# A second MLP as 2x2 block products with seven multiplications, in superblocks of 768 tokens, with streamed weights

## The chip, the cores and the metric

The kernel runs on one core of one Trainium2 chip. The core has a matrix engine (TensorE: PE in the profile, its weight loads PEld), three elementwise engines (VectorE: DVE, ScalarE: ACT, GpSimd: POOL) and a queue engine (SyncE: SP) from which all DMAs of this kernel are issued. The metric is the device time of one execution in microseconds (us).

## The reference: a retention layer and two MLPs

Retention over 4 batches, 8 heads, 576 positions and 64 dimensions gives a 2304 x 512 matrix. Two MLPs follow, all in float32:

```python
def _moe_ref(x, w_in, w_out):            # x: 2304 x 512, w_in: 512 x 2048, w_out: 2048 x 512
    h = np.maximum(x @ w_in, 0.0)
    return (h * h @ w_out).astype(np.float32)

def _moe2_ref(x, w_in, w_out):
    h = x @ w_in
    relu6 = np.clip(h + 3.0, 0.0, 6.0)
    g = h * relu6 / 6.0
    return (g @ w_out).astype(np.float32)
...
    x = _moe_ref(x=x, **moe_kwargs)
    return _moe2_ref(x=x, **moe2_kwargs)
```

## The kernel before

Every float32 operand of the MLPs is held as two float32r parts, a high one (a rounding cast) and a low one (the rest), and a product is three matmuls: high by high, high by low, low by high. Both MLPs run over the 2304 tokens in five blocks of 512 or 384 (`BLOCKS`), and within a block over 16 slices `f` of 128 hidden features. A step is one `(ph, blk, f)`: `h_part` makes one 128-feature slice of h (12 matmuls, 4 input slices by 3), ACT and DVE turn it into g (`r` at L459 to L463, `g` at L466 to L469), and `a_part` adds the slice's share of the output into PSUM (`acc`, L491 in the first MLP, L493 in the second). The loop over `steps` issues `h_part` of the next step ahead of `a_part` of this one, so that PE has 12 matmuls to do while g is made. The order on every engine is the order in which the program is written; each engine takes its instructions strictly in that order.

The first MLP (`ph` 0) reads its input from SBUF, where `first_*`, `scores` and `values` (the retention, in chunks of 128 tokens, one chunk in four or five steps) have put it for the next block. Its result goes to DRAM (`x1`), and `load_x1` brings it back, block by block, for the second MLP (`ph` 1). Weights come in once per MLP: `load_w` (512 KB per DMA), `scale_w` on ACT (L128, L129) and `narrow_w` on DVE (L144, L145), which turn the 64-bit numbers into float32, and `split_w` (cast on ACT, rest on POOL or DVE, L156 and L158). The 32 weight tiles of an MLP stay in SBUF for all its blocks. The second MLP's weights are prepared during the last block of the first and the first block of the second.

In the second MLP the five blocks take 16 x 12 matmuls each for h (960, moving 512 or 384 columns) and 16 x 3 for each of the 18 groups of 128 tokens (864, moving 512 columns). Each `a_part` result is scaled by 1/6 on its way out (L514 on DVE, L516 on ACT) and stored (L520).

## Time and profile before

| | |
|---|---|
| time, median of 3 runs | 875.69 us (875.45 to 875.77) |
| profiled execution, first to last instruction (the page gives no other time for it) | 874.3 us |
| PE busy | 860.0 us (98%), 5356 matmuls |
| DVE, ACT, POOL busy | 458.5, 227.8, 95.9 us |
| DMA queue of SP | 67.33 MB |

The page divides the span into 40 slices and gives the busy tenths of each engine; a table by stage gives the same in us. The chain that ended last is followed back from the last instruction to what released each step. The profiled execution is one, its span is 1.4 us under the median of the runs.

### The profile page before, as it was taken

To read this page: it belongs to the slowest core of one execution; us is meant where nothing else is said; L and a number is where in the kernel's file an instruction comes from. 1 tells how busy PE (TensorE), PEld (TensorE's weight loads), DVE (VectorE), ACT (ScalarE), POOL (GpSimd) and SP (SyncE) were. 2 spreads that over 40 slices of the span, in tenths; PEclk is the share of its full clock that TensorE was granted. 3 is DMA by queue.
4 is the path that set the end of the run, shared out by engine and by line. 5 is a ranking of instruction groups with operands and counts; after the bars stand their busy time and mean duration, and the time that the engine had idled before them with its cause. 6 is when DMAs were issued, how large, how long until landed. Compare 5 with 4: busy or idle time off the path is not lost.

```text
span 874.3 us, 12831 instructions
## 1 busy us (share of the span) xinstructions
PE 860.0 (98%) x5356; PEld 741.5 (85%) x5356; DVE 458.5 (52%) x778; ACT 227.8 (26%) x394; POOL 95.9 (11%) x86
## 2 busy tenths in 40 slices
PE   8899999999999999999999999999999999999998
PEld 7677779999888899998888998888888888888996
DVE  6788875445444355445788785335333533344333
ACT  2666641111111111114555642111111111111111
POOL 3455560101111011000000000000000000000000
PEclk9999999999999999999999999999999999999999
DMA  9956212112111021016565300100010001001001
GB/s 340 315 203 236 97 49 98 49 49 85 49 49 46 3 96 50 2 38 206 199 213 175 97 13 13 61 1 13 28 57 1 13 35 41 1 10 47 2 1 37
DMA packets 29130, 68.15 MB, mean 78 GB/s; under 512 B 2832, under 2 KB 12176, under 8 KB 29072
## 3 DMA queue, kind: packets, MB, share of 16 engines
q1 hardware_dynamic: 29072, 67.33, 23.2%
q8 instruction: 42, 0.69, 0.3%
q14 instruction: 16, 0.13, 0.1%
HBM read 57.88 MB, written 9.44 MB: 77 GB/s over the span
## 4 chain that ended last, share of the span: by engine, by line
PE 86%; DMA 5%; DVE 3%; issue 2%; POOL 1%; ACT 1%; SPq 0%; POOLq 0%; DVEq 0%; ACTq 0%
PE h L449 41%; PE acc L493 23%; PE acc L491 19%; DMA raw<-w_dram 3%; DMA q<-qk_dram 2%; PE o L420 1%; PE o L410 1%; PE sc L338 1%; POOL w L158 1%; DVE wt L145 1%; DVE wt L144 1%; DVE r L460 0%; PE sc L353 0%; ACT g L466 0%; POOL q L309 0%
## 5 line engine op out<-in xcount | busy, mean ns | idle before, releaser
L449 PE MATMUL h<-x,w 128*128 128x512 f32 (+2 forms) x1932 | 423.4, 367 | 5.8 <-ACT w L156 3.7
L449 PEld LDWEIGHTS h<-x,w 128*128 128x128 f32 x1932 | 351.4, 188 | 56.6 <-ACT w L156 5.7
L491 PE MATMUL acc<-g,w 128*128 128x512 f32 (+1 forms) x960 | 213.7, 371 | 1.0 <-ACT g L466 1.0
L493 PE MATMUL acc<-w,g 128*128 128x512 f32 x864 | 210.2, 391 | 0.3 <-DVE ev L514 0.3
L491 PEld LDWEIGHTS acc<-g,w 128*128 128x128 f32 x960 | 173.5, 188 | 24.3 <-ACT g L466 1.4
L493 PEld LDWEIGHTS acc<-w,g 128*128 128x128 f32 x864 | 161.5, 188 | 33.2 <-DVE ev L514 0.8
L463 DVE SCALAR_TENSOR_TENSOR r<-r,h 128x512 f32<-128x512 f32 (+1 forms) x80 | 50.7, 634 | 203.1 <-ACT r L462 203.0
L462 ACT ACTIVATE r<-h,con 128x512 f32<-128x512 f32 (+1 forms) x80 | 51.7, 646 | 311.3 <-PE h L449 305.8
L460 DVE TENSOR_TENSOR r<-r,h 128x512 f32<-128x512 f32 (+1 forms) x80 | 50.6, 632 | 148.9 <-ACT r L459 148.8
L469 DVE TENSOR_TENSOR g<-r,g 128x512 fp32r<-128x512 f32 (+1 forms) x160 | 108.2, 676 | 16.2 <-ACT g L466 11.2
L459 ACT ACTIVATE r<-h 128x512 f32<-128x512 f32 (+1 forms) x80 | 44.2, 552 | 240.6 <-PE h L449 233.7
L468 DVE CAST g<-r 128x512 fp32r<-128x512 f32 (+1 forms) x144 | 65.1, 452 | 14.6 <-DVE r L460 0.5
L145 DVE CUSTOM_DVE_ANT_0 wt<-raw,wt 128x1024 uint16<-128x1024 uint16 x64 | 47.1, 737 | 4.5 <-DVE wt L144 0.6
L158 POOL TENSOR_TENSOR w<-wt,w 128x512 fp32r<-128x512 f32 x32 | 42.7, 1339 | 53.0 <-ACT w L156 43.9
L128 ACT ACTIVATE raw<-raw 128x512 f32<-128x512 f32 x64 | 42.8, 669 | 2.6 <-DMA raw<-w_dram 2.6
L129 ACT ACTIVATE raw<-raw 128x512 int32<-128x512 uint32 x64 | 42.8, 669 | 0.0
L309 POOL TENSOR_TENSOR q<-q,con 128x512 f32<-128x512 f32 x13 | 18.2, 1402 | 175.7 <-issue 115.7
L156 ACT ACTIVATE w<-wt 128x512 fp32r<-128x512 f32 x50 | 30.8, 627 | 13.3 <-DVE wt L145 13.1
L144 DVE TENSOR_SCALAR wt<-raw 128x512 int32<-128x512 int32 x64 | 30.3, 474 | 0.1
L158 DVE TENSOR_TENSOR w<-wt,w 128x512 fp32r<-128x512 f32 x32 | 21.3, 685 | 0.0
L466 ACT ACTIVATE g<-r 128x512 fp32r<-128x512 f32 x16 | 10.1, 633 | 29.9 <-DVE r L460 29.9
L514 DVE TENSOR_SCALAR ev<-acc 128x512 f32<-128x512 f32 (+1 forms) x18 | 11.8, 658 | 9.1 <-DMA x<-ev 4.1
(47 smaller groups left out, 273.1 us busy)
## 6 DMA issues: line engine op xcount, KB each, us to landing
raw<-w_dram SPq DMA_DIRECT2D x64, 512.0 KB, 5.8
q<-qk_dram SPq DMA_DIRECT2D x17, 512.0 KB, 3.7
kv<-kv_dram SPq DMA_DIRECT2D x30, 256.0 KB, 4.9
out_dram<-ev SPq DMA_DIRECT2D x18, 256.0 KB, 2.1
x<-ev SPq DMA_DIRECT2D x12, 256.0 KB, 2.1
x1r<-x SPq DMA_DIRECT2D x12, 256.0 KB, 4.6
kv<-kv_dram SPq DMA_DIRECT2D x3, 512.0 KB, 7.9
x<-ev SPq DMA_DIRECT2D x8, 192.0 KB, 1.9
```

Of the source, the lines that this page charges most:

```text
L128: nc.scalar.activation(high, high, AF.Prelu, scale=2.0**-112, alpha=-(2.0**32))
L145: nc.vector.tensor_tensor(ti, ti, low, ALU.add)
L158: eng.tensor_tensor(w[:, 1, :], t, w[:, 0, :].bitcast(F32), ALU.subtract)
L449: nc.tensor.matmul(hp[:, ts], w[:, wi, c * P : (c + 1) * P], x[:, xi, c, ts], start=k == 0, stop=k == 3 * NC - 1,)
L459: nc.scalar.activation(r, hp[:, :nb], AF.Relu)
L460: nc.vector.tensor_tensor(r, r, hp[:, :nb], ALU.mult)
L462: nc.scalar.activation(r, hp[:, :nb], AF.Relu, bias=con3)
L463: nc.vector.scalar_tensor_tensor(r, r, 6.0, hp[:, :nb], ALU.min, ALU.mult)
L468: nc.vector.tensor_copy(g[:, 0, :nb], r)
L469: nc.vector.tensor_tensor(g[:, 1, :nb], r, g[:, 0, :nb].bitcast(F32), ALU.subtract)
L491: nc.tensor.matmul(acc[d][:, :nb], wt[:, sl], gt, start=first, stop=stop)
L493: nc.tensor.matmul(acc[d], gt[:, sl], wt, start=first, stop=stop)
```

## The change

Only the second MLP is computed in another way; the first keeps its blocks, steps and matmuls.

- **Seven products.** The tokens are taken in 3 superblocks of 768 (`SUPERS`), each as two halves of 384 (`HALF`). Of both products of the second MLP the operands are cut in 2x2 blocks, seven combinations of each operand are formed, seven block products made, and the four output blocks are sums of those (`ORDER` is the order 1, 6, 7, 5, 2, 4, 3). Two of the sums are made in PSUM, by letting products 2, 4 and 3 add on a bank that already holds 1, 7 or 5.
- **First product.** Per superblock there are 8 pairs `j` of 128 hidden features; per `j` seven products of 6 matmuls, moving 384 columns (L977). Per `j` ACT copies one product out, DVE makes five sums with a PSUM operand (L872), ACT and DVE make the four gated blocks (`relu3` L905, `gate` L908), and POOL four sums of those (`pool_op` L911), which are the seven left operands of the second product (`aop_1` to `aop_7`), kept for all 8 `j`.
- **Second product.** It starts when all 8 `j` are done (h is ahead of it): per superblock 7 x 8 steps of 9 matmuls, moving 256 columns (L1026). `a_cast` (ACT) and `a_low` (DVE, L925) split one 128 x 384 operand per step into six rotating tiles; `merge` and `emit` read the sums out (L939 and the lines behind) and store them.
- **Weights.** Instead of staying in SBUF, the second MLP's combined weights are prepared during the first MLP: 32 `unit`s, each a load (two DMAs), scaling on ACT, narrowing and four sums on DVE, one cast of 128 x 896 on ACT, one subtraction of 128 x 896 on DVE, and two stores of 448 KB to DRAM, in pieces of 512 B. A unit is spread over two steps (`unit_work`), from step 14 of the first block to the end of the first MLP. For every superblock they are read again through a ring of seven 512 KB tiles (`ring_load`): 32 loads for the first product (every fourth 256 KB) and 28 for the second. A tile's next load waits for PE to be done with it.
- **Input.** `x_stages` makes the seven combinations of x1 and their high and low parts for a superblock: for the first one in the last 8 steps of the first MLP, for the others during the second product before.
- **Beside that**, in the first MLP the cast of g to its high part is ACT's in all blocks (before: DVE's after the first block), its low part is emitted behind the unit's DVE work, retention chunks are loaded one ahead instead of two (one buffer instead of two), and a mask is loaded by a DMA of its own.
- The order in the second MLP is set by a list of model times: `at(t, ...)` puts an operation on a heap, and `run(now)` emits what is due as PE's matmuls are written.

```diff
-BLOCKS = (
-    [(512, "xa"), (384, "xb"), (512, "xa"), (384, "xb"), (512, "xa")],
-    [(384, "xb"), (512, "xa"), (512, "xc"), (512, "xa"), (384, "xb")],
-)
+BLOCKS = [(512, "xa"), (384, "xb"), (512, "xa"), (384, "xb"), (512, "xa")]
...
+SUPERS, HALF = 3, 384
...
+ORDER = (1, 6, 7, 5, 2, 4, 3)
...
+RING = 7
...
+    def unit_load(n):
+        i, j, u = n // (2 * NJ), n // 2 % NJ, n % 2
+        raw = upool.tile([P, 2, 2, P, 2], I32, tag="raw", bufs=1, name=f"uraw_{n}")
...
+    def unit_narrow(n):
+        raw = units[n]
+        low, high = raw[:, :, 0], raw[:, :, 1]
+        t = upool.tile([P, 7, P], F32R, tag="seven", bufs=2, name=f"seven_{n}")
+        ti = t[:, :4].bitcast(I32).rearrange("p s n -> p (s n)")
+        nc.vector.tensor_scalar(ti, high, 3, None, ALU.logical_shift_left)
+        nc.vector.tensor_tensor(ti, ti, low, ALU.add)
...
+    def unit_low(n):
+        t, hi = units[n]
+        nc.vector.tensor_tensor(t, t.bitcast(F32), hi.bitcast(F32), ALU.subtract)
+
+    def unit_store(n, x):
...
+        if i == 0:
+            nc.sync.dma_start(w_in_hl[j][:, :, x, cols], part)
+        else:
+            nc.sync.dma_start(w_out_hl[:, :, j, x, cols].rearrange("s p n -> p s n"), part)
+
+    def unit_work(i, slot):
+
+        n, odd = divmod(i, 2)
...
+        if slot == 0 and not odd:
+            on(1, unit_narrow)
+            on(0, unit_load)
+            on(2, unit_store, 0)
+        elif slot == 0:
+            on(2, unit_low)
+            on(2, unit_store, 1)
+        elif not odd:
+            on(1, unit_combine)
+        else:
+            on(0, unit_scale)
+            on(1, unit_cast)
...
+    def ring_load(n):
+        s, i, a, b = ring[n]
+        p = p1c if n % RING == RING - 1 else p1a
+        t = p.tile([P, 2, 2, HALFD], F32R, tag=f"r{n % RING}", name=f"ring_{n}")
...
+            for i, q in enumerate(ORDER):
+                run(now)
+                w = wring[s, 0, j, i // 2][:, i % 2]
+                x = x_ops[q]
...
+                    nc.tensor.matmul(
+                        bank[q],
+                        w[:, wi, u * P : (u + 1) * P],
+                        x[:, u, xi, :],
+                        start=k == 0 and q not in (2, 4, 3),
+                        stop=k == 5,
+                        skip_group_check=q in (2, 4, 3),
+                    )
...
+                    at(now + 2.0, pool_op, 5, 7, 4, ALU.add, j)
+                    at(now + 2.1, pool_op, 7, 1, 7, ALU.subtract, j)
+                    at(now + 2.2, pool_op, 6, 5, 1, ALU.subtract, j)
+                    at(now + 2.3, pool_op, 3, 2, 6, ALU.subtract, j)
...
+                    for m, (g, wi) in enumerate(((0, 0), (0, 1), (1, 0))):
+                        nc.tensor.matmul(
+                            o,
+                            sp[:, g, rows],
+                            w[:, k % 2, wi, :],
```

PE, early in the second MLP before: `h` is a PSUM tile, `x_1_0` the input block, `w_1_f_0` and `w_1_f_1` the two weight tiles of slice f, `acc` the output's PSUM tiles.

```order
L449 MATMUL h_1_0_1_4356<-x_1_0_3999,w_1_1_0_3784 128x384 x12
L493 MATMUL acc_1_0_0_4383<-w_1_0_1_3739,g_1_0_0_4314 128x512 x4
L493 MATMUL acc_1_0_1_4384<-w_1_0_1_3739,g_1_0_0_4314 128x512 x2
L493 MATMUL acc_1_0_0_4383<-w_1_0_1_3739,g_1_0_0_4314 128x512 x2
L493 MATMUL acc_1_0_1_4384<-w_1_0_1_3739,g_1_0_0_4314 128x512
```

PE, the first `j` of the second MLP now: `z0` to `z7` are the eight PSUM banks, `xop_q` the combinations of x, `ring_n` the streamed weights, `spl_s_q_k` the split left operands.

```order
L977 MATMUL z6_4746<-xop_1_4374,ring_0_4428 128x384 x6
L977 MATMUL z7_4747<-xop_6_4375,ring_0_4428 128x384 x6
L977 MATMUL z4_4744<-xop_7_4376,ring_1_4476 128x384 x6
L977 MATMUL z5_4745<-xop_5_4377,ring_1_4476 128x384 x6
L977 MATMUL z6_4746<-xop_2_4378,ring_2_4519 128x384 x6
L977 MATMUL z4_4744<-xop_4_4379,ring_2_4519 128x384 x6
L977 MATMUL z5_4745<-xop_3_4380,ring_3_4571 128x384 x6
```

And PE where the first superblock passes from the first product to the second:

```order
L977 MATMUL z2_4742<-xop_4_4379,ring_30_5153 128x384 x6
L977 MATMUL z3_4743<-xop_3_4380,ring_31_5174 128x384 x6
L1026 MATMUL z6_4746<-ring_32_5192,spl_0_1_0_5233 128x256 x6
L1026 MATMUL z7_4747<-ring_32_5192,spl_0_1_0_5233 128x256 x3
L1026 MATMUL z6_4746<-ring_32_5192,spl_0_1_1_5249 128x256 x6
L1026 MATMUL z7_4747<-ring_32_5192,spl_0_1_1_5249 128x256 x3
```

The two kinds of matmuls that alternated every 12 or 9 now stand in two long runs: 8 x 7 groups of the first kind, then 7 x 8 of the second, and the second kind moves 256 columns instead of 512.

DVE, early in the second MLP before (weights of `ph` 1 still in preparation; `r` reads PSUM), one step:

```order
L158 TENSOR_TENSOR w_1_11_0_4449<-wt_1_11_0_4416,w_1_11_0_4449 128x512
L144 TENSOR_SCALAR wt_1_11_1_4452<-raw_1_11_1_4152 128x512
L145 ISA wt_1_11_1_4452<-raw_1_11_1_4152,wt_1_11_1_4452 128x1024
L463 SCALAR_TENSOR_TENSOR r_1_0_4_4479<-r_1_0_4_4479,h_1_0_4_4466 128x384
L468 CAST g_1_0_4_4482<-r_1_0_4_4479 128x384
L469 TENSOR_TENSOR g_1_0_4_4482<-r_1_0_4_4479,g_1_0_4_4482 128x384
```

DVE now, one `j` of the first product (`held` tiles keep the partial sums, `aop_q` the gated blocks):

```order
L872 TENSOR_TENSOR held0_4710<-z7_4747,held0_4710 128x384
L872 TENSOR_TENSOR held1_4711<-z4_4744,held0_4710 128x384
L872 TENSOR_TENSOR held0_4710<-z5_4745,held1_4711 128x384
L908 SCALAR_TENSOR_TENSOR aop_4_4718<-aop_4_4718,held0_4710 128x384
L908 SCALAR_TENSOR_TENSOR aop_1_4713<-aop_1_4713,z6_4746 128x384
L872 TENSOR_TENSOR held1_4711<-z4_4744,held0_4710 128x384
L872 TENSOR_TENSOR held0_4710<-z5_4745,held0_4710 128x384
L908 SCALAR_TENSOR_TENSOR aop_2_4717<-aop_2_4717,held1_4711 128x384
L908 SCALAR_TENSOR_TENSOR aop_7_4715<-aop_7_4715,held0_4710 128x384
```

Weight preparation, casts and subtractions have left this place; nine operations on 384 columns per `j` have come, six with a PSUM operand and three (`aop_4`, `aop_2`, `aop_7`) with SBUF operands alone.

DVE, two steps of the second block of the first MLP, before:

```order
L460 TENSOR_TENSOR r_0_1_5_1578<-r_0_1_5_1578,h_0_1_5_1565 128x384
L468 CAST g_0_1_5_1581<-r_0_1_5_1578 128x384
L469 TENSOR_TENSOR g_0_1_5_1581<-r_0_1_5_1578,g_0_1_5_1581 128x384
L460 TENSOR_TENSOR r_0_1_6_1609<-r_0_1_6_1609,h_0_1_6_1596 128x384
L468 CAST g_0_1_6_1612<-r_0_1_6_1609 128x384
L469 TENSOR_TENSOR g_0_1_6_1612<-r_0_1_6_1609,g_0_1_6_1612 128x384
```

And now (`uraw`, `seven` and `uhi` are the unit's raw weights, its seven combinations and their high parts):

```order
L567 TENSOR_SCALAR seven_2_1612<-uraw_2_1508 128x512
L568 ISA seven_2_1612<-uraw_2_1508,seven_2_1612 128x1024
L482 TENSOR_TENSOR r_0_1_5_1632<-r_0_1_5_1632,h_0_1_5_1619 128x384
L575 TENSOR_TENSOR seven_2_1612<-seven_2_1612 128x128
L576 TENSOR_TENSOR seven_2_1612<-seven_2_1612 128x128
L577 TENSOR_TENSOR seven_2_1612<-seven_2_1612 128x128
L578 TENSOR_TENSOR seven_2_1612<-seven_2_1612 128x128
L490 TENSOR_TENSOR g_0_1_5_1635<-r_0_1_5_1632,g_0_1_5_1635 128x384
L593 TENSOR_TENSOR seven_1_1505<-seven_1_1505,uhi_1_1597 128x896
L482 TENSOR_TENSOR r_0_1_6_1669<-r_0_1_6_1669,h_0_1_6_1656 128x384
L490 TENSOR_TENSOR g_0_1_6_1672<-r_0_1_6_1669,g_0_1_6_1672 128x384
```

The two casts have gone to ACT; a unit's seven operations stand between the steps' own, the first two of them ahead of a step's `r`.

## Rows read from the trace of the kernel before

**Rows 1.** Page: busy time, share of the span and instructions of each engine.

```profile
PE 860.0 (98%) x5356; PEld 741.5 (85%) x5356; DVE 458.5 (52%) x778; ACT 227.8 (26%) x394; POOL 95.9 (11%) x86
```

**Rows 2.** Page: the chain that ended last, by engine.

```profile
PE 86%; DMA 5%; DVE 3%; issue 2%; POOL 1%; ACT 1%; SPq 0%; POOLq 0%; DVEq 0%; ACTq 0%
```

**Rows 3.** Stages: window, length, PE, PEld, DVE, ACT, POOL busy, clock, DMA, GB/s.

```profile
0.00:24.00 24.00, 21.04 (x250) 19.16 (x251) 14.95 (x24) 6.58 (x12) 7.69 (x12) 1.00 0.93 347
...
124.00:190.50 66.50, 66.50 (x618) 63.52 (x610) 30.72 (x55) 11.22 (x22) 9.87 (x10) 1.00 0.26 80
...
478.70:869.90 391.20, 391.20 (x1800) 333.17 (x1800) 171.52 (x312) 74.18 (x120) 0.00 (x0) 1.00 0.08 26
```

**Rows 4.** Timeline of PE: start us, length, line; boundary of the MLPs, end.

```profile
471.24 2.27 PE L449 MATMUL h<-x,w 128*128 128x384 f32 x12
...
476.11 2.27 PE L449 MATMUL h<-x,w 128*128 128x384 f32 x12
...
865.55 4.36 PE L493 MATMUL acc<-w,g 128*128 128x512 f32 x18
```

**Rows 5.** The chain in order of time, second MLP: start us, us, what.

```profile
485.26 2.10 PE h L449 x12
487.36 2.08 PE acc L493 x9
...
560.77 2.72 PE h L449 x12
563.49 2.72 PE acc L493 x12
```

**Rows 6.** Timeline of PEld, 25 to 27 us: 256-column matmuls.

```profile
24.94 2.21 PEld L449 LDWEIGHTS h<-x,w 128*128 128x128 f32 x18 [0.71 <-POOL w L158]
```

**Rows 7.** One window of L449 alone: length, PE, PEld busy, clock, DMA, GB/s.

```profile
25.20:27.60 2.40, 2.40 (x21) 2.40 (x21) 1.00 1.04 387
```

**Rows 8.** Groups by shape: busy us, mean ns of one, idle before.

```profile
L145 DVE CUSTOM_DVE_ANT_0 wt<-raw,wt 128x1024 uint16<-128x1024 uint16 x64 | 47.1, 737 | 4.5 <-DVE wt L144 0.6
...
L144 DVE TENSOR_SCALAR wt<-raw 128x512 int32<-128x512 int32 x64 | 30.3, 474 | 0.1
...
L309 POOL TENSOR_TENSOR q<-q,con 128x512 f32<-128x512 f32 x13 | 18.2, 1402 | 175.7 <-issue 115.7 <-PE sc L338 60.0
L460 DVE TENSOR_TENSOR r<-r,h 128x384 f32<-128x384 f32 x32 | 17.7, 554 | 73.2 <-ACT r L459 73.2
...
L536 DVE TENSOR_TENSOR x<-x1r,x 128x384 fp32r<-128x384 f32 x8 | 4.5, 558 | 0.3
...
L221 POOL TENSOR_TENSOR kv<-kv,con 128x512 f32<-128x512 f32 x4 | 4.4, 1089 | 9.5 <-DMA kv<-kv_dram 9.5
```

**Rows 9.** Timeline of DVE and POOL: an SBUF-only operation beside POOL.

```profile
199.26 1.27 POOL L309 TENSOR_TENSOR q<-q,con 128x512 f32<-128x512 f32 x1 [15.44 <-issue]
199.48 1.27 DVE L468 CAST g<-r 128x384 fp32r<-128x384 f32 x1
```

**Rows 10.** The same, an operation with a PSUM operand beside POOL.

```profile
41.76 2.54 POOL L158 TENSOR_TENSOR w<-wt,w 128x512 fp32r<-128x512 f32 x2 [6.60 <-ACT w L156]
...
42.20 0.69 DVE L460 TENSOR_TENSOR r<-r,h 128x512 f32<-128x512 f32 x1 [1.41 <-ACT r L459]
```

**Rows 11.** Timeline of SP's queue: DMAs of 128 and 256 pieces, time to issue.

```profile
205.91 0.33 SPq L191 DMA_DIRECT2D q<-qk_dram  x1
206.35 1.26 SPq L197 DMA_DIRECT2D kv<-kv_dram  x2
```

**Rows 12.** Page: what the DMAs moved, by slice; us from issue to landing.

```profile
GB/s 340 315 203 236 97 49 98 49 49 85 49 49 46 3 96 50 2 38 206 199 213 175 97 13 13 61 1 13 28 57 1 13 35 41 1 10 47 2 1 37
...
x<-ev SPq DMA_DIRECT2D x12, 256.0 KB, 2.1
```

**Rows 13.** Timeline of the last us: ACT and DVE read the last sums out.

```profile
869.26 1.29 ACT L516 ACTIVATE ev<-acc 128x512 f32<-128x512 f32 x2 [2.93 <-PE acc L493]
...
869.89 0.69 DVE L514 TENSOR_SCALAR ev<-acc 128x512 f32<-128x512 f32 x1 [1.92 <-ACT ev L516]
```

More of the change, by code (lines that the diff above doesn't have):

```diff
@@ L88, in retention_moe_kernel @@
     nc = tc.nc
[L89 to L97 removed]
+    nblk = len(BLOCKS)
@@ L481, in a_part @@
             ]
-            accs[ph, blk] = [two[d // 2][:, d % 2, :] for d in range(n_acc)]
+            accs[ph, blk] = [two[d // 2][:, d % 2, :] for d in range(NC)]
         acc = accs[ph, blk]
@@ L486, in mm @@
         def mm(d, wi, gi, first, stop):
[L487 to L493 removed]
+            wt = w[:, wi, d * P : (d + 1) * P]
+            nc.tensor.matmul(acc[d][:, :nb], wt, g[:, gi, :nb], start=first, stop=stop)
         if last:
[L496 removed]
+            for d in range(NC):
                 mm(d, 0, 0, False, False)
@@ new lines, in retention_moe_kernel @@
+        if half < i <= half + RING - 1:
+            ring_load(i - half - 1)
+        if i > half:
+            k = i - half
+            if k < len(x_first[0]):
+                for st in x_first:
+                    do(st[k])
+        a_part(ph, blk, f)
+        if f == NF - 1 and blk + 1 < nblk:
+            evict(blk)
+            unit_work(i - NF + 2, 1)
+    unit_work(len(steps) - NF + 1, 1)
+    for v in range(len(steps) - NF + 2, len(steps) - NF + 4):
+        unit_work(v, 0)
+        unit_work(v, 1)
@@ new lines, in retention_moe_kernel, with at, run @@
+    left.close()
+    p1c = pool(ctx, "p1c", 1, side="left")
+    held = [
+        upool.tile([P, 2, HALF], F32, tag=tag, bufs=1 + (tag == "seven"), name=f"held{k}")
+        for k, tag in enumerate(("raw", "seven", "seven"))
+    ]
+    a_ops = {
+        q: p1c.tile([P, NJ, HALF], F32R, tag=f"a{q}", name=f"aop_{q}") for q in ORDER
+    }
+    heap = []
+    def at(t, fn, *a):
+        heapq.heappush(heap, (t, len(seen), fn, a))
+        seen.append(0)
+    seen = []
+    def run(t):
+        while heap and heap[0][0] <= t:
+            _, _, fn, a = heapq.heappop(heap)
+            fn(*a)
@@ new lines, in retention_moe_kernel, with ring_done @@
+    ring_load(RING - 1)
+    evict(nblk - 1)
+    psum.close()
+    ps1 = pool(ctx, "ps1", 1, space=bass.MemoryType.PSUM)
+    z = [ps1.tile([P, 512], F32, tag=f"z{k}", name=f"z{k}") for k in range(8)]
+    used = [0]
+    def ring_done(t):
+        n = used[0] + RING
+        used[0] += 1
+        if n < len(ring):
+            at(t, ring_load, n)
+    t_in = 6 * (HALF + 32) / 2400.0
+    t_out = 3 * NJ * NTT * (HALFD + 32) / 2400.0
+    now = 0.0
+    act = nc.scalar.activation
+    tt = nc.vector.tensor_tensor
```

441 lines of the change are left out of this document (320 added, 121 removed).

## The prediction

> **What bounds the kernel now.** I read the busy shares first: PE is busy for 860.0 of 874.3 us, DVE for about half, ACT and POOL for less [rows 1]. "Busy" of PE includes pipelining, so I asked the chain of waits next: 86% of it is PE, 5% DMA, and the DMAs lie in the start [rows 2]. Then the stages: from 478.7 to 869.9 us PE is busy in every us, DVE in 171.5 of 391.2, DMA at 8% [rows 3]. The second MLP is thus bound by PE alone, and by the rate at which it starts matmuls. The boundary: the second MLP's first 12 matmuls (471.24 us) stand ahead of the first MLP's last 12; from 476.11 us on all is second MLP [rows 4]. Taking those 12 out (2.10 us, rows 5), the first MLP would have ended at 474.0; the last matmul ends at 865.55 + 4.36 = 869.9. The second MLP costs **395.9 us**.
>
> **The rate of a matmul.** In the chain 12 matmuls of 512 columns take 2.72 us, 226.7 ns each; 12 of 384 columns take 2.10, 175 ns; 9 of 512 between those take 2.08, 231 ns [rows 5]. For 256 columns there is one short stretch: 18 weight loads from 24.94 us in 2.21 us, the last lasting about 0.19, so 2.02 / 17 = 119 ns, and 2.40 us of full windows with 21 of them, at a DMA rate of 387 GB/s and full granted clock [rows 6, 7]. Columns at 2.4 GHz would be 213, 160 and 107 ns: each matmul has 12 to 18 ns beyond its columns, and the weight load of 128 columns is hidden also behind 256. By these rates before is 576 x 226.7 + 384 x 175 (h) + 576 x 226.7 + 288 x 231 (output) = 394.9 us, 1.0 short of the 395.9.
>
> **What the change removes and adds on PE.** After, the first product is 3 x 8 x 7 x 6 = 1008 matmuls of 384 columns, 176.4 us; the second 3 x 7 x 8 x 9 = 1512 of 256. I take 122 ns for these: the stretch shows 119, and the blocks with 384 tokens show up to 4 ns on top of the best rate (231 against 226.7), which bounds it by 124. That is 184.5 us (179.9 to 187.5). With the same 1.0 of remainder: 361.9 us. **Gain 34.0 us** (31 to 38.6). Columns fall by an eighth, 884,736 to 774,144 (46.1 us at 2.4 GHz), but matmuls rise from 1824 to 2520, which gives a quarter of that back.
>
> The Trainium skill says otherwise of the fixed part: its page "TensorE: Matmul & The Clock Gate", section "Back-to-back issue gap", gives a warm gap of N / 2.4 + 2.5 ns. By it before would be 373 us and the second MLP after 329, a gain of 44 and a time some 10 us under mine. The rows at full clock do not agree (226.7 ns where it has 215.8). I keep the rows; what remains of the rule is rival D.
>
> **Does PE stay fed in the second MLP?** Terms by engine, none on the path if it holds:
> - *DVE in the first product.* Per `j` (42 matmuls, 7.35 us) nine operations of 128x384 at 554 ns = 5.0 us [rows 8]. Three read SBUF alone. Beside a POOL operation such an operation waits until POOL's is over (cast of 384: 1.27 us, ending when POOL's 1.27 ends), one with a PSUM operand does not (0.69 beside POOL) [rows 9, 10]. POOL's four per `j` cost 0.8 (1089 ns for 512 columns, scaled) to 1.05 us each (1402, scaled) [rows 8], 3.3 to 4.2 us. If all three waited a whole one: 5.0 + 3.2 = 8.2; if none: 5.0. They come mostly when POOL is between groups, so I take 6. PE's nearest need is product 4, which adds on product 7's bank three groups (2.1 us less one sum of 0.55) after it was made: about 1.5 us of slack.
> - *Second product.* Per step of 9 matmuls (1.1 us) one cast on ACT and one subtraction on DVE (558 ns [rows 8]), six steps ahead; with x's parts (22 x 0.56) and six sums DVE has about 50 of 61 us. Covered; without cover each step would show up to 0.5 us.
> - *The weight stream.* 60 loads are 29.4 MB per superblock, with x and the output 32.5 MB in 120.6 us: 270 GB/s. The start moves 347 at a DMA share of 0.93 [rows 3], so the share would be 0.72. The ring is seven loads deep, six groups of two products (12 us) ahead of need. SP issues them between output stores that wait for DVE or ACT for about 1.2 us; covered by those 12.
> - *The last superblock.* Two read-outs follow the last matmul on DVE (0.69 + 0.41) where before ACT's and DVE's ran beside each other [rows 13]: +0.4.
>
> **What moves into the first MLP.** There, between 124.00 and 190.50 us, DVE is busy 30.7 of 66.5, ACT 11.2, DMA 26% [rows 3], so there is room, but the queues are in order. A unit costs DVE, over two steps, 0.47 + 0.74 [rows 8], four sums of 128 columns (some 0.27 each, scaled down from 558 for 384) and one subtraction of 896 (1.2, scaled up): 3.5 us; a cast of g leaves in each step. DVE goes to about 3.4 us per step of 4.2 (24 x 175) plus retention. *Added waits:* the unit's narrowing waits for the raw load, for ACT's scaling and, since `seven` has two buffers, for the store of the unit two before. Behind it in DVE's queue stands `r` of the next step, and for g of that step PE waits. SP issues 128 pieces in 0.33 us and 256 in 0.63 [rows 11], 2.3 ns per piece; a store has 896: 2.1 us to issue, and 2.1 to land by the x stores [rows 12], against one step until its tile is wanted. In 384-token blocks that is nearly the whole step. The wait hides if g is still in time (one step after h, some 1.5 us to spare). Nearest rows say between 0 and 0.5 us per step there (32 steps): 0 to 15 us; a gain is excluded since PE is already gapless there. I take **+3**. The retention's single buffer and the later loads of weights in the first block lie in that bound too.
>
> **Boundary.** In the last seven steps x's combinations (22 x 0.56 us) join the unit work: DVE 4.8 of 5.4 us per step, and product 6, one group in, waits for their last parts. 0 to 4 us, I take **+1.5**. The clock stays granted in all this [rows 3].
>
> **The sum**, against the profiled execution: 874.3 - 34.0 + 3.0 + 1.5 + 0.4 = 845.2 us; it stood 1.4 under the median of the runs (875.69), so **846.6 us**. With the bounds of rate and small terms and phase costs up to 8: 839 to 853.
>
> **The rivals.**
> - *A. The unit work stalls the first MLP.* `seven`'s store is not back when DVE wants the tile, `r` slips behind it, PE waits for g. For: SP's 2.1 us per store and a step of 4.2 us. Against: the low part of g is wanted only after eight matmuls, and 512-token steps have 1.3 us more. Price: 0.25 to 0.6 us in each of the 32 + some steps, 8 to 21 us above mine's 3: 853 to 867.
> - *B. DVE and POOL bind the first product.* If the three SBUF-only operations wait for whole POOL operations, DVE has 8.2 us per `j` against 7.35; 24 x 0.85 = 20 us: 867 (to 875 if POOL's operations lengthen too). Against: the order puts those three operations largely where POOL is idle.
> - *C. Slower: the stream binds.* Before, no DMA traffic ran for long at the rate wanted: 340 GB/s only in the first slice, 203 and 236 in the third and fourth [rows 12]. The point from which the second MLP is no faster than before is 97.5 MB / 396 us = 246 GB/s. At 236 it takes 413 us, 51 above mine: **898 us**. Against: those slices ended because the loads did, and the first 24 us hold 347 [rows 3], with 512 KB loads. The Trainium skill speaks for C: its page "DMA: Bandwidth & Descriptors", section "Bandwidth", asks for transfers of 1 MiB or more for three quarters of the peak, and the ring's are half that. The trace's 347 GB/s came with loads of at most 512 KB, several in flight, so the trace bears C out little.
> - *D. Less beyond the columns.* In long runs of one shape the part beyond the columns could shrink, and nothing else cost anything: with 119 ns for 256 columns and 173 for 384 (2.08 us for 12) the second MLP takes 355 us, 41 less than before: 835 to 838. Against: the runs of 512 columns in rows 5 are of one shape too and show 226.7.
> - That the change does not do what it says is hardly open: the counts of matmuls stand in the program.
>
> **Chances.** Forecast 0.64, A 0.17, B 0.10, C 0.07, D 0.02. The range holds the forecast, A, and B in part: 837 to 868. About 0.2% (1.8 us) is what a measurement of this kernel can tell from no change. Faster by more: 0.64 + 0.17 + 0.10 + 0.02, less 0.01 for B's far end = 0.92; within: 0.01; slower: C, 0.07.
>
> **What would show it.** The chain of waits in the second MLP: groups of 6 matmuls of 384 columns in 1.05 us and of 9 of 256 in 1.07 to 1.12, without pieces of DMA or DVE between. The first-MLP stages: PE busy throughout, the second MLP beginning by 479. A: PE's wait list names g, and DVE's names the store of `seven`. B: DVE busy over 90% in the first product, POOL beside it, PE waiting for `held`. C: PE waiting for `ring` loads, DMA share at 0.9. I am wrong in the main term if the matmuls of 256 columns come slower than 124 ns with nothing waiting.

## The result, and the profile after

| us | before | after |
|---|---|---|
| median of the runs | 875.57 (874.79 to 875.77, 4 runs) | 846.24 (844.25 to 848.27, 4 runs) |
| ratio to before, 95% interval | | 0.9669 (0.9648 to 0.9689) |
| profiled execution, its span | 874.3 | 842.4 |
| first MLP ends, second begins | 474.0 | 483.15 |
| second MLP, to the end of the last matmul | 395.9 | 355.2 |

The change makes the kernel faster by 29.3 us; 846.6 was forecast. The total is right, but two terms in it are wrong, one either way: the second MLP gives back 40.7 us instead of 34.0, and the first MLP with the boundary pays 9.1 instead of 4.5. The experiments are about those two terms. Two of the four executions, 847.83 and 848.27 us, had a mean granted clock of 0.995, the other two, 844.25 (the profiled one) and 844.64, of 1.0 and 0.999, so the profile shows the change at its shortest; none of the two longer ones was profiled. (Below, the second MLP is taken from its first matmul's start to its last one's, 354.9 us here.)

The page of the changed kernel, busy time and the chain by engine, beside [rows 1] and [rows 2]:

```profile
PE 823.3 (98%) x6052; PEld 758.6 (90%) x6052; DVE 578.1 (69%) x1034; ACT 385.7 (46%) x710; POOL 203.9 (24%) x182
...
PE 77%; DMA 6%; issue 5%; DVE 5%; POOL 3%; ACT 2%; SPq 2%; DVEq 0%; POOLq 0%; ACTq 0%
```

DVE, ACT and POOL work more than before, but PE is still busy for 98%. PE's share of the chain fell from 86% to 77%: more of the chain now lies with DVE, SP, POOL and "issue" (time in which an engine waited for nothing that the profile shows). By stage, as in [rows 3] (window, length, busy us and instructions of PE, PEld, DVE, ACT, POOL, granted clock, DMA share, GB/s): the second to fifth block of the first MLP, then the second MLP.

```profile
133.00:217.00 84.00, 80.45 (x762) 76.92 (x761) 51.46 (x104) 34.33 (x61) 8.97 (x9) 1.00 0.64 181
217.00:314.00 97.00, 97.00 (x680) 79.13 (x679) 56.84 (x105) 37.77 (x62) 12.54 (x13) 1.00 0.58 168
314.00:397.00 83.00, 80.88 (x767) 77.32 (x766) 52.33 (x103) 34.49 (x61) 10.51 (x10) 1.00 0.66 190
397.00:483.00 86.00, 86.00 (x375) 69.89 (x375) 55.01 (x108) 41.37 (x72) 0.00 (x0) 1.00 0.60 185
483.20:838.10 354.90, 354.90 (x2521) 354.90 (x2519) 258.86 (x463) 166.27 (x331) 107.53 (x96) 1.00 0.81 269
```

In the second MLP PE is busy for all of the 354.9 us shown, at full granted clock. In the first MLP it is not: PE lacks 3.6 us in the second block and 2.1 in the fourth, the two with 384 tokens. The boundary (timeline of PE: start us, length, line) has no gap at all; the first matmul of the second MLP, at 483.15, follows on a group that begins at 482.22:

```profile
482.22 1.09 PE L508 MATMUL acc<-g,w 128*128 128x512 f32 x4
483.15 0.69 PE L977 MATMUL z<-xop,ring 128*128 128x384 f32 x3
```

Of what DVE waits for in the whole kernel (engine, line, releaser: us in total, times, longest), these are the rows on the store of `seven`; the second view is the chain of waits around 199 us, in the second block:

```profile
DVE seven L567 <- DMA w_in_hl<-seven: 16.0, 4, 5.9
...
DVE seven L567 <- DMA w_out_hl<-seven: 10.1, 3, 5.1
```

```profile
191.61 7.37 DMA w_in_hl<-seven
...
199.11 0.75 DVE seven L567
...
199.98 0.88 DVE seven L568
200.86 0.46 DVE r L482
```

A store of `seven` issued at 191.61 us is back after 7.37. DVE's narrowing (L567) of the unit two later wants that tile and starts only at 199.11; behind it in DVE's queue stands `r` (L482, 200.86); behind that ACT's cast of g, and PE waits for g 1.36 us, at 201.94. Why the store was late stands in SP's queue (start us, time to issue, line):

```profile
188.54 0.52 SPq L600 DMA_DIRECT2D w_in_hl<-uhi  x1
189.16 0.60 SPq L215 DMA_DIRECT2D q<-qk_dram  x1
189.85 1.67 SPq L221 DMA_DIRECT2D kv<-kv_dram  x2
191.61 0.62 SPq L600 DMA_DIRECT2D w_in_hl<-seven  x1
```

The retention's load of its next chunk, 1 MB in three DMAs, was issued just ahead of it. The median landing of the stores of `seven` is 4.2 us (to `w_in_hl`) and 3.8 (to `w_out_hl`); this one took 7.4. In the second to fifth block ten of 30 such stores stand right behind a chunk's load: they land in 4.7 to 7.4 us, the 20 others in 3.5 (median).

### The profile page after: what moved, and what is told of

Read it like the earlier page. It is cut to its first block, busy times and chain, and to the rows that moved or that the text cites. A ratio compares the mean times of both kernels' runs of the same rounds, so it can differ in the third digit from the quotient of the medians.

```text
span 842.4 us, 15782 instructions
## 1 busy us (share of the span) xinstructions
PE 823.3 (98%) x6052; PEld 758.6 (90%) x6052; DVE 578.1 (69%) x1034; ACT 385.7 (46%) x710; POOL 203.9 (24%) x182
## 4 chain that ended last, share of the span: by engine, by line
PE 77%; DMA 6%; issue 5%; DVE 5%; POOL 3%; ACT 2%; SPq 2%; DVEq 0%; POOLq 0%; ACTq 0%
PE z L1026 21%; PE z L977 21%; PE acc L508 16%; PE h L472 16%; DMA w_in_hl<-seven 3%; POOL w L177 2%; DMA raw<-w_dram 1%; PE o L444 1%; PE o L434 1%; DVE r L482 1%; DMA w_out_hl<-seven 1%; ACT g L484 1%; DVE seven L568 1%; POOL q L333 1%; SPq L221 1%
## 5 line engine op out<-in xcount | busy, mean ns | idle before, releaser
L472 PE MATMUL h<-x,w 128*128 128x512 f32 (+2 forms) x972 | 214.2, 368 | 4.5 <-ACT w L176 2.5
L472 PEld LDWEIGHTS h<-x,w 128*128 128x128 f32 x972 | 175.0, 188 | 31.7 <-ACT w L176 4.3
L1026 PE MATMUL z<-ring,spl 128*128 128x256 f32 x1512 | 180.4, 282 | 0.0
L1026 PEld LDWEIGHTS z<-ring,spl 128*128 128x128 f32 x1512 | 180.3, 191 | 0.0
L911 POOL TENSOR_TENSOR aop<-aop,aop 128x384 f32<-128x384 f32 x96 | 107.5, 1131 | 294.7 <-DVE aop L908 184.7
L977 PE MATMUL z<-xop,ring 128*128 128x384 f32 x1008 | 175.6, 335 | 0.0
L977 PEld LDWEIGHTS z<-xop,ring 128*128 128x128 f32 x1008 | 175.1, 188 | 0.1
L925 DVE TENSOR_TENSOR spl<-aop,spl 128x384 fp32r<-128x384 f32 x168 | 99.3, 606 | 33.6 <-ACT spl L921 32.2
L921 ACT ACTIVATE spl<-aop 128x384 fp32r<-128x384 f32 x168 | 86.3, 522 | 59.9 <-PE z L1026 55.8
L482 DVE TENSOR_TENSOR r<-r,h 128x512 f32<-128x512 f32 (+1 forms) x80 | 50.5, 631 | 77.9 <-ACT r L481 77.3
L905 ACT ACTIVATE aop<-held,con 128x384 f32<-128x384 f32 x72 | 44.5, 617 | 108.4 <-DVE held L872 107.8
L872 DVE TENSOR_TENSOR held<-z,held 128x384 f32<-128x384 f32 x120 | 66.5, 554 | 29.6 <-PE z L977 27.6
L908 DVE SCALAR_TENSOR_TENSOR aop<-aop,held 128x384 f32<-128x384 f32 x72 | 49.7, 690 | 17.8 <-ACT aop L905 16.2
L567 DVE TENSOR_SCALAR seven<-uraw 128x512 int32<-128x512 int32 x32 | 15.7, 492 | 33.5 <-DMA w_in_hl<-seven 16.0
```

Source lines behind the costliest of these rows:

```text
L472: nc.tensor.matmul(hp[:, ts], w[:, wi, c * P : (c + 1) * P], x[:, xi, c, ts], start=k == 0, stop=k == 3 * NC - 1,)
L482: nc.vector.tensor_tensor(r, r, hp[:, :nb], ALU.mult)
L872: fn(*a)
L911: nc.gpsimd.tensor_tensor(f32(o, j), f32(a, j), f32(b, j), op)
L921: act(t[:, 0, :], f32(q, k), AF.Copy)
L925: tt(t[:, 1, :], f32(q, k), t[:, 0, :].bitcast(F32), ALU.subtract)
```

## Experiments

**Theory.** The second MLP is bound by the rate at which PE starts matmuls, and that rate is better than forecast; the first MLP's 9.1 us are mostly stalls behind a few stores of `seven` that the chunk's load delays. **Rivals:** the stalls come from the unit work on DVE and ACT itself (A, and the retention's own waits); DVE and POOL (B) or the stream of weights (C) hold the second MLP back after all. Each ratio is against the kernel before on the same chip.

**1. The changed kernel again.** No edit.

> The changed kernel once more, as the measure for the others on this chip. All theories: 844 to 849 us, first MLP's last matmul about 483 us from the start (before: 474.0 without the second MLP's first 12 matmuls), second MLP about 355 us. If the difference between its executions (844.3 and 848) is chance in the first MLP's stalls, the second MLP is the same length in a slow and a fast profile.

Measured: 846.98 us, ratio 0.9671 (0.9651 to 0.9691). In the profiled execution (span 844.6) the second MLP is again 354.9 us; the second and the fourth block are 84.7 and 85.2 us instead of 83.9 and 83.4. What differs between these two profiled executions is thus the first MLP's stalls.

**2. The chunk's load behind the store.** In the second to fourth block the load of the next chunk moves by one slot, from ahead of the store of `seven` to behind it:

```diff
                 elif slot == (3 if blk == 0 else 2):
                     values(c, xs[0, blk + 1], j * P)
+                    if blk == 0:
+                        load_chunk(c + 1)
+                elif blk and slot == 3:
                     load_chunk(c + 1)
```

> In blocks 1 to 3 the retention's chunk load is issued one step later, behind the store of seven instead of ahead of it. Theory 1 with the chunk load as the reason that the store is late (7.4 us from issue to landing where others take 4): the two long waits (5.9 and 5.1 us) shrink below 2, the stalls of PE that follow them (about 5 us) go, time 841 to 843. If the store is late for its own length: unchanged, or slower by the chunk's later arrival (0 to 4 us).

Measured: 836.69 us, ratio 0.9565 (0.9548 to 0.9582), 9.6 us under the change (10.3 under its repeat on the same chip; 7.5 between the profiled executions). SP's queue at the same place of this kernel, DVE's waits for the stores, and its windows (columns as above) over the second and fourth block and the second MLP:

```profile
188.12 0.52 SPq L600 DMA_DIRECT2D w_in_hl<-seven  x1
188.69 0.65 SPq L215 DMA_DIRECT2D q<-qk_dram  x1
```

```profile
DVE seven L567 <- DMA w_in_hl<-seven: 0.8, 1, 0.8
DVE seven L567 <- DMA w_out_hl<-seven: 0.4, 1, 0.4
```

```profile
132.00:212.00 80.00, 80.00 (x762) 76.90 (x761) 53.04 (x104) 34.47 (x61) 9.28 (x9) 1.00 0.69 192
...
309.00:390.00 81.00, 81.00 (x771) 77.87 (x770) 53.45 (x103) 35.02 (x62) 11.82 (x10) 1.00 0.70 196
...
475.70:830.60 354.90, 354.90 (x2520) 354.90 (x2519) 259.00 (x463) 166.28 (x331) 107.52 (x96) 1.00 0.82 269
```

DVE's waits for these stores fall from 26 us to 1.2, PE has no gap in the second to fifth block, and the second MLP is the same. The unit work on DVE and ACT is all still there. The place of one load in SP's queue costs the change 9.6 us. That is more than expected (841 to 843 us): most of the short waits went with the two long ones, and the stores of `seven` now land in 3.5 us (median). Of the 7.5 us between the profiled executions 6.6 lie in the second and fourth block; the rest is where the first block ends, which differs by 0.9 us although its order is the same.

**3. Only the stores.** All unit work is taken out, and one tile of zeros is stored 64 times at the same places (its definition is left out of the cut).

```diff
         if slot == 0 and not odd:
-            on(1, unit_narrow)
-            on(0, unit_load)
             on(2, unit_store, 0)
         elif slot == 0:
-            on(2, unit_low)
             on(2, unit_store, 1)
-        elif not odd:
-            on(1, unit_combine)
-        else:
-            on(0, unit_scale)
-            on(1, unit_cast)
...
```

> All unit work (loads, scaling, narrowing, sums, cast, subtraction) is left out of the first MLP; only the 64 stores remain, from a tile of zeros, so the second MLP multiplies by zero weights. Theories 1 and 2: the first MLP ends at 474 to 475.5, time 837 to 839. Theory 3 (traffic): matmuls of 512 columns still every 233 ns in blocks 2 and 4, first MLP 476 to 478, time 839 to 841. If the cast of g on ACT or the single retention buffer costs something by itself, the stalls in blocks 1 and 3 stay.

Measured: 836.96 us, ratio 0.9561 (0.9548 to 0.9574). Without any unit work the kernel is no faster than with all of it and the load moved (836.69). So the work itself costs nothing that shows; only the wait did. The blocks are also alike: 79.9, 97.3, 80.8 and 85.6 us here, 79.9, 97.3, 80.8 and 85.7 in experiment 2. Against before (79.8, 96.2, 80.7, 84.6) the two blocks with 512 tokens remain 1.1 us longer each, which is thus neither the unit work nor the stall; experiments 8 to 10 find it.

**4 and 5. A third tile of `seven`, and its control.** The third tile takes away what the narrowing waits for. To make room, the pool `tmpp` went from four tiles to two; the control has this alone. (Other tiles that share the tag `seven`, `held` among them, get three as well; that part of the edit is left out here.)

```diff
-    tmpp = pool(ctx, "tmpp", 4, side="left")
+    tmpp = pool(ctx, "tmpp", 2, side="left")
...
-        t = upool.tile([P, 7, P], F32R, tag="seven", bufs=2, name=f"seven_{n}")
+        t = upool.tile([P, 7, P], F32R, tag="seven", bufs=3, name=f"seven_{n}")
...
```

> Three buffers of the tile seven instead of two (and, to make room, two of the small output tiles instead of four). Theory 1 (the unit's narrowing waits in DVE's queue for the store of the unit two before, and r, g and PE wait behind it): DVE's waits of L567 for stores (26 us, longest 5.9) go, PE's stalls at 185.6, 201.9, 207.9, 362.7, 364.6, 368.9 us (6.1 us together) go, the first MLP ends at about 477, time 840 to 842. Theory 2 (it is the unit's own DVE and ACT work, whatever it waits for): unchanged, 846 within 1.5. Theory 3 (matmuls of 512 columns start every 233 ns instead of 227 because of the DMA traffic): unchanged.

Measured: 848.52 us, ratio 0.9695 (0.9681 to 0.9709), which alone would speak against the theory. But the stalls in the middle of the second and fourth block were gone, and others had come: PE waits 0.3 to 1.0 us near the starts of four blocks (each 0.5 to 1.3 us longer than in experiment 2), and the second MLP takes 362.9 us.

> The pool of temporary tiles has two tiles instead of four, alone: the control for the run with three tiles of `seven`, which had this change beside it. Theory: the gaps of 0.7 to 1.3 us at the starts of blocks and the second MLP of 362.9 us (355 otherwise) in that run come from here: both come back, together with the stalls behind the store of `seven` (kernel about 855). Rival: the second MLP's 8 us came from the third tile that `held` got with `seven`: then the second MLP is 355 here, the kernel about 847.

Measured: 860.9 us in one run, second MLP 363.4. The control's waits of PE, and ACT's timeline at the start of its second MLP:

```profile
PE z L977 <- ACT held L872: 5.8, 1, 5.8
...
PE acc L508 <- DVE ev L529: 3.9, 4, 1.9
```

```profile
500.47 0.60 ACT L531 ACTIVATE ev<-acc 128x512 f32<-128x512 f32 x1 [8.11 <-DMA x<-ev]
500.96 0.48 ACT L872 ACTIVATE held<-z 128x384 f32<-128x384 f32 x1
```

The first row is most of the second MLP's 8 us: ACT's second read-out of the first MLP waits 8.11 us for a tile of `tmpp` whose store is under way, the first sum of the first `j` (L872) stands behind it, and PE waits 5.8 for that. About 2 us more are the clock. It fell to 0.50 (1.2 GHz) during this wait, and 16 matmuls of 384 columns take 4.80 us right behind it (columns as in the windows above) where 16 x 173.7 ns are 2.8:

```profile
501.80:506.60 4.80, 4.80 (x16) 4.80 (x16) 3.17 (x7) 1.35 (x3) 0.00 (x0) 0.50 0.81 273
```

The other row of PE is the starts of blocks. So both came from the room, not from `held`. Against the kernel before or the change the run with three tiles is not a clean test of the theory. Against its control it is one: with two tiles in `tmpp` in both, the third tile of `seven` takes 12.4 us off (860.9 to 848.5), the second MLP begins at 478.9 us instead of 491.4, and DVE's waits for the stores of `seven`, 32 us in the control, are gone.

**6. POOL's additions on DVE** (rival B).

```diff
     def pool_op(o, a, b, op, j):
-        nc.gpsimd.tensor_tensor(f32(o, j), f32(a, j), f32(b, j), op)
+        nc.vector.tensor_tensor(f32(o, j), f32(a, j), f32(b, j), op)
```

> The four additions per inner block that GpSimd does in the first product are done by VectorE. VectorE then has 9 x 0.554 + 4 x 0.56 = 7.2 us per inner block of 42 matmuls (7.29 us at 173.7 ns), with no GpSimd work beside it. Theory (VectorE had room, 5.0 to 6 of 7.3 us, and GpSimd only kept it): VectorE is busy in over 95% of the first product and the slack of TensorE's bank is gone in part: 0 to 0.5 us of wait per inner block, the second MLP 355 to 367 us. Rival B's premise (sharing with GpSimd costs VectorE as much as GpSimd takes away from it, so VectorE had been near 8 us per inner block): no loss, the second MLP within 1 us of 355, and the operations of VectorE that now take 690 ns on the mean fall to 554.

Measured: 855.76 us in one run, second MLP 365.6, 10.6 more. PE's waits in the second MLP, of which the changed kernel has none, and DVE's groups there (us busy, mean ns of one; then idle before):

```profile
PE z L977 <- DVE held L872: 5.3, 18, 0.7
...
L911 DVE TENSOR_TENSOR aop<-aop,aop 128x384 f32<-128x384 f32 x96 | 51.2, 553 | 1.7
L908 DVE SCALAR_TENSOR_TENSOR aop<-aop,held 128x384 f32<-128x384 f32 x72 | 40.1, 558 | 17.8 <-ACT aop L905 15.4
```

In the changed kernel:

```profile
L911 POOL TENSOR_TENSOR aop<-aop,aop 128x384 f32<-128x384 f32 x96 | 107.5, 1131 | 294.7 <-DVE aop L908 184.7
...
L908 DVE SCALAR_TENSOR_TENSOR aop<-aop,held 128x384 f32<-128x384 f32 x72 | 49.7, 690 | 17.8 <-ACT aop L905 16.2
```

Beside POOL, L908 takes DVE 72 x 132 ns = 9.5 us more over the whole second MLP; the work that POOL takes off it is 51.2. Sharing does lengthen DVE's operations on SBUF alone, as B says, but by 0.13 us each, not by a whole operation of POOL. Without POOL's help, DVE is late now and then: by the starts of its matmuls PE has 38 gaps in the first product, 10.4 us, 0.43 per inner block.

**7. The stream of weights** (rival C), in two kernels. First, every load issued twice:

> Every load of the stream of weights is issued twice, into the same tile: 58.8 MB and 3.1 of x and the output per superblock of 118.3 us, 523 GB/s if nothing gave way. Theory (the stream had room, but not that much): the second MLP becomes bound by the DMA engines at about the 347 GB/s of the start, up to the 387 of the one window: 61.9 MB / 0.347 to 0.387 = 160 to 178 us per superblock, the second MLP 480 to 535 us instead of 355, the kernel 967 to 1022 us, TensorE waiting for the ring and the DMA share at 0.9 or more. Rival C's premise (a sustained stream of such loads gets about 236 GB/s): 262 us per superblock, the second MLP 787 us. If the kernel hardly slows (under 900), the stream had more than twice the room and its rate never was in question.

Measured: 1418.07 us, second MLP 918.7, longer than either side expected. This decides nothing on the rate: in a window of 400 us (600 to 1000 us) SP waits 316.8 us for the first copy of a load, so that the second may go into the same tile:

```profile
SPq L784 <- DMA ring<-w_out_hl: 167.8, 38, 6.4
SPq L779 <- DMA ring<-w_in_hl: 149.0, 38, 4.9
```

SP then issues a second copy and the next tile's first copy together and waits again, so two loads of 512 KB are in flight, not seven: 918.7 / 180 = 5.1 us for each two. What was measured is the time of two loads. (The page's clock stands at 7 to 8 tenths there, between the levels of 1.2 and 2.4 GHz, with PE idle before every tile.) Then the loads alone:

> Computes nothing of the reference: the loads of the stream of weights alone, 180 loads (88.1 MB, 512 KB each but for 24 of 256) from the same arrays in DRAM, filled with zeros first, into the same seven tiles, each tile's next load waiting only for the one before it; no other engine works. The run with every load issued twice had the second copy wait for the first and so did not measure what the stream can carry; this does. Theory (the stream had room: 347 GB/s in the first 24 us of the kernel before, 249 to 340 in the slices of the second MLP after, where TensorE never waited for it): 88.1 MB in at most 254 us, at 347 GB/s or more. Rival C's premise: the rate is about 236 GB/s, 373 us, and the break-even is 246, 358 us.

Measured, the windows of the stream (length, DVE busy, POOL busy, clock, DMA share, GB/s) and its loads on the page (KB each, us to landing):

```profile
100.00:310.00 210.00, 0.00 (x0) 0.00 (x0) 1.00 1.04 398
```

```profile
ring<-w_out_hl SPq DMA_DIRECT2D x84, 512.0 KB, 8.9
```

398 GB/s, 221 us for the 88.1 MB, against 269 that the second MLP moves and 246 at C's break-even. C falls: loads of 512 KB, seven in flight, keep the DMA engines busy throughout (share 1.04 as the view gives it), and the kernel uses 0.81 of them. The Trainium skill's "DMA: Bandwidth & Descriptors", section "Bandwidth", asks for 1 MiB per DMA for three quarters of the peak; the row here does not bear this out for a queue that keeps seven loads in flight.

**8 and 9. The rate of matmuls by themselves.** In the changed kernel the rate had two levels with nothing waiting. In the chain of waits (start us, us, what) one group of 12 matmuls in the first half of the third block takes 2.80 us, 233.3 ns each, and one in the second half 2.72, 226.7; in the second product 43 take 5.16, 120 ns each:

```profile
239.86 2.80 PE acc L508 x12
...
298.49 2.72 PE h L472 x12
...
552.95 5.16 PE z L1026 x43
```

By the addresses that the program gives its tiles (no trace shows them), the slow half is that whose weight tiles lie on the other side of SBUF, at another offset in a line of 256 bytes than the moving operand. Two kernels hold nothing but streams of matmuls on zeros, at chosen offsets; the first has 8 at each of 16 x 16 places, the second 40 at each of 16 distances.

> This kernel computes nothing of the reference: it holds only streams of 8 matmuls on zeros (512, then 256 columns, at all 16 x 16 places in steps of 32 bytes of the moving operand and of the weights in a 512-byte line of SBUF; then 384 columns at 8 x 8 places), and writes zeros. In the traces a matmul of 512 columns starts every 226.7 ns where the weights lie at 160 of 512 bytes in SBUF and every 233.3 where they lie at 480 (the moving operand at 160 both times); one of 256 columns every 113 to 114 ns in the 216 cases where the moving operand lies at 160 and every 120 in the 1295 where it lies at 480 (weights at 480). Theory: the place in the 512-byte line (of one operand, or of the one against the other) sets the time beyond the columns, in steps of 6.7 ns. It expects a map with at least two levels per shape, 226.7 for (moving 160, weights 160) and 233.3 for (160, 480) at 512 columns, 113.3 for (160, 480) and 120 for (480, 480) at 256. Rival: it is not the place but what the other engines and queues read and write at that time (which buffers are in use goes with the place): then, with all of them idle here, one level per shape in the whole map.

> Computes nothing of the reference (streams of matmuls on zeros, zeros written): 40 matmuls in a row at each of 16 distances, in steps of 16 bytes, of the moving operand's address from the weights' address, modulo 256 bytes, for 512, 256, 384 and 128 columns. In the map of short streams (8 matmuls) the time followed this distance alone, and the last matmuls of a stream stood at 226 to 227 ns for 512 columns at distances 0 and 64 and 231 to 238 elsewhere; at 113 ns for 256 columns at distance 192 and 115 to 120 elsewhere; at 173 ns for 384 columns, with 171 at 192. Theory (each distance has a settled level): the second half of each stream repeats these, 233.3 at distance 192 for 512 columns, 113.3 at 192 and 120 at 0 for 256, 173.3 at 0 for 384. Rival (what the short streams show is only their start): in the second half all distances come to one level per shape.

The first map follows the distance of the two addresses modulo 256 bytes, not the 512 that were expected: wherever the operands lie, groups of 512 columns at one distance have the same mean to 0.5 ns, but for the first ones of a row of the map. Those are the only ones that come after another distance than the rest, and there the same distance can give another mean (226.7 and 230.1 ns at distance 0). What ran before thus already counts here; experiments 10 and 11 come back to it. The second, the second half of each stream in the chain: 512 columns at distances 0 and 192, 256 columns at 0, 112 and 192, 384 columns at 0 and 192:

```profile
44.64 4.76 PE z L121 x21
...
155.98 4.90 PE z L121 x21
...
190.92 2.52 PE z L121 x21
...
224.07 2.38 PE z L121 x21
...
247.58 2.38 PE z L121 x21
...
267.50 3.64 PE z L121 x21
...
351.31 3.71 PE z L121 x21
```

That is 226.7 and 233.3 ns for 512 columns, 120.0, 113.3 and 113.3 for 256, 173.3 and 176.7 for 384. The levels are those of the kernel, with every other engine idle: they go with the addresses of the operands, and what else runs on the chip is not needed for them. The best distance is another for each shape: 0 and 240 for 512 columns, 112 and 192 for 256, 0 and several others for 384.

**10. Two unused tiles of 64 bytes per partition**, on the kernel of experiment 2:

```diff
     gpool = pool(left, "gpool", 2, side="left")
+    gpool.tile([P, 16], F32, tag="pad", bufs=1, name="padg")
...
         n = len(splits) % NSPL
+        if len(splits) == 0:
+            p1a.tile([P, 16], F32, tag="pad", name="pads")
```

> The changed kernel with the load of a chunk behind the store (as in the run that moved it), and two unused tiles of 64 bytes: one ahead of g, the first MLP's x and the left half of its weights, which brings the distance of moving operand from weights to 0 of 256 bytes for all its matmuls of 512 columns (192 for those with weights in the right half without it), and one between the ring and the parts of a, which brings it to 192 for all 1512 matmuls of 256 columns (0 for 1295 of them without it). Theory (the distance sets the rate): 1295 x (119.8 - 113.3) = 8.4 us less in the second MLP, 346.5 instead of 354.9; 1.1 and 1.3 us less in the third and fifth block; 836.7 - 10.8 = 825.9 us, 825 to 828. Rival (the rates go with which buffers are in use or with the other engines, not with the distance): 836.7.

Measured: 832.42 us, ratio 0.951 (0.9498 to 0.9523). The third and fifth block fall from 97.3 and 85.7 to 96.3 and 84.5 us, about as expected; in the chain the group of 12 now takes 2.72. The second MLP falls by 2.2 us, not 8.4: all 1512 matmuls of 256 columns stand at 117.8 ns.

```profile
240.38 2.72 PE acc L509 x12
...
559.95 20.14 PE z L1032 x171
```

So distance 192 does not always give 113.3. In the run without these tiles a ring tile at 192 came after six at 0, and stood at 113.3; here all are at 192, and a slower pattern holds from the first matmul to the last.

**11. One ring tile of seven at distance 0**, the others at 192, on the kernel of experiment 10:

```diff
+    p1c.tile([P, 16], F32, tag="pad", name="padr")
     ring_load(RING - 1)
```

> As the run with the two unused tiles of 64 bytes, and a third one ahead of the ring's seventh tile, so that the distance of the moving operand from the weights in the second product is 192 of 256 bytes for six ring tiles of seven and 0 for the seventh. In the run with all seven at 192 every matmul of 256 columns stood at 117.8 ns from the first to the last, in a pattern that repeats every 15 matmuls; in the run before it the tile at 192 stood at 113.3 within four matmuls after tiles at 0, which stood at 120. Theory (there are two rhythms at distance 192, and the one before decides which is taken): entered from the 120 of the seventh tile, the six others stand at 113.3 to 113.6: the mean is (6 x 113.6 + 119) / 7 = 114.4 ns, 1512 x 3.4 = 5.1 us less than 117.8, with at most 0.5 us given back in the first product, where that tile's weights come to distance 192: second MLP 348, the kernel 832.4 - 4.7 = 827.7 us. Rival (a tile at 192 holds 113.3 for its first 18 matmuls or so alone, or only that one tile's address gives it): the mean stays at 117.5 to 118, the kernel at 832 to 833.

Measured: 827.79 us (827.35 to 828.35), ratio 0.9458 (0.9445 to 0.9471); second MLP 348.6. The six tiles stand at 113.3, entered from the seventh's 120 (here 36 matmuls in 4.08 us, and a mean over 20.13 us of 114.4):

```profile
559.92 4.08 PE z L1033 x36
...
559.92 20.13 PE z L1033 x176
```

The same run shows the other pattern too. At its first entry into the second product, behind matmuls of 384 columns, 28 matmuls take 3.30 us, 117.8 ns each:

```profile
531.17 3.30 PE z L1033 x28
```

They stay there until the seventh tile has passed, and the same tiles stand at 113.3 from then on; this repeats in all three superblocks. So two patterns exist at the same addresses, and what ran before decides between them. This is the fastest of the kernels, 18.5 us under the change as it was made: 9.6 from one load's place in a queue, 8.9 from 192 unused bytes per partition.

## Why the prediction was right in the sum, and where its steps were not

- **PE alone binds the second MLP: right.** PE is busy throughout and waits for nothing in it, and DVE, POOL and the stream all stay under their limits. DVE was put at 6 of 7.35 us per `j`; the window of 483 to 523 us has 30.1 busy of 40, so 5.5. The stream was put at a DMA share of 0.72; it is 0.81 at 269 GB/s. One reading under it was wrong: in [rows 9] DVE's cast ends at 200.75 us, 0.22 after POOL's operation, so the row does not show that DVE waits until POOL is done; the mean cost beside POOL was 0.13 us (experiment 6).
- **The gain of 34.0 us: the mechanism right, the size off by 7.** The step that failed is "I take 122 ns for these". The short stretch in the trace showed 119 [rows 6], and I moved away from it because some groups of 512 columns were 4 ns over their best [rows 5]. Measured: the page's busy time gives 180.4 us / 1512 = 119.3, starts to starts 119.0, and 173.7 for 384 columns where I had 175: 1512 x 3.0 + 1008 x 1.3 = 5.8 us, and the remainder of 1.0 that the prediction carried along did not come back. The 231 that I took as a bound is a level of 512 columns that goes with addresses; it does not carry over in size or sign to another shape and other tiles (experiments 8 and 9).
- **Rival D's second MLP, 355 us, is the one measured.** It was given 0.02 on the ground that long runs of 512 columns show 226.7. After the change some do, others show 233.3; the 119 of the one 256-column stretch was the better witness for 256 columns. D's time, 835 to 838, is that of the kernel with the load moved: 836.7.
- **The skill's rule was rightly set aside.** N / 2.4 + 2.5 ns (the Trainium skill, "TensorE: Matmul & The Clock Gate", section "Back-to-back issue gap", which gives it for a single matmul by itself and 131 ns at 512 columns for a stream) would be 162.5 and 109.2 ns; measured are 173.3 at best and 113.3 at best, and 226.7 at best for 512 columns in a stream. With the best level of either shape the second MLP would be 1008 x 173.3 + 1512 x 113.3 ns = 346 us, not 329.
- **The first MLP's +3: the mechanism right, the size off.** The chain named (store of `seven`, narrowing, `r`, g, PE) is what the trace of after shows link by link. Three sizes under it were wrong. The issue was scaled from 2.3 ns per piece to 2.1 us per store [rows 11]; it took 0.5 to 0.6. The landing was taken at 2.1 from another store [rows 12]; it took 3.5 where nothing of the chunk was ahead of it, and 4.7 to 7.4 behind the chunk's load. And the stall was spread over 32 steps as an even chance, while it came in a few, behind the stores that the chunk's load delayed. The prediction noted that SP is in order, and did not list what stands ahead of the store. Measured: the second and fourth block 4.0 and 2.6 us longer than with the load moved.
- **A term that was missing:** 2.2 us in the third and fifth block from the offset of the weight tiles; the program put a new pool above them. Experiment 10 gets it back (1.0 and 1.2 us).
- **Boundary +1.5: wrong, 0.** x's combinations were in time; the tail, put at +0.4, is 4.0 us from the last matmul's end to the end of the span, where before had 4.4.
- **The sum:** 845.2 by the steps against 842.4 in the profiled execution and 844.6 in that of experiment 1. Put right: 874.3 - 40.7 + 6.6 + 2.2 + 0 - 0.4 = 842.0, 0.4 short of 842.4. The total came out because the two errors were of opposite sign. That is luck: either error alone, 6.7 us in the second MLP or 4.6 in the first MLP and the boundary, would have stood in the total.
- **Rivals A, B, C.** A has the right chain and the wrong frequency: a few waits, 6.6 us in all. (Its range should begin at 855: 846.6 + 8.) B has the right contention (690 against 558 ns), and none of it reached PE. C falls by experiment 7.

## What to carry to other kernels

When an edit adds DMAs to a queue that already serves the loop, write down what stands ahead of each in that queue and how many bytes it moves: a load of 1 MB ahead of a store, in ten steps of the first MLP, took back a quarter of what the change can gain, and moving it by one slot cost nothing. Take a rate from the stretch with the same shape, however short, rather than from a longer one of another shape. Where PE is gapless and binds, look at the offsets of its two operands modulo 256 bytes: 192 unused bytes per partition were worth 1% here.

## What the chip showed that was not expected

- A matmul's time beyond its columns goes with the distance of its operands' SBUF addresses modulo 256 bytes: for 512 columns of fp32r 226.7 to 234.8 ns, for 256 columns 113.3 to 120.2, for 384 columns 173.3 to 179.9, with nothing waiting and nothing else running. For 128 columns it does not: 111.4 to 111.8 at every distance, so 256 columns take hardly longer than 128.
- At one distance the time can have two lasting values (113.3 and 117.8 ns for 256 columns at 192), and what ran just before decides which. Why is open: no run here looks inside the engine. Nor was it tried whether the same holds for other types of data or other orders of the weights.
- A store of 896 pieces takes SP 0.5 to 0.6 us to issue, less than the 0.63 of a load of 256 pieces [rows 11]: the number of pieces does not scale the issue time across these two forms.
- A store of 448 KB that lands in 3.5 us (median of 20) takes 4.7 to 7.4 (ten of ten) when 1 MB of loads was issued in the 2.3 to 2.9 us ahead of it, with a DMA share of 0.58 to 0.66 in the blocks.
